# Third batch's attention eight slots earlier, second batch's queries loaded one slot earlier, and memory traffic ordered behind TensorE steps

## The chip, the cores and the metric

One Trainium2 chip, of which the kernel uses one core. The metric is the device time of one execution in microseconds (us), the median of three runs for the kernel before. The engines are named as in the profile: PE is TensorE with PEld its weight loads, DVE is VectorE, ACT is ScalarE, POOL is GpSimd, and SP is SyncE, which here only issues DMAs.

## The reference

Three stages follow one another; all of it is float32, with the weights of the second stage handed over as 64-bit numbers.

```python
q_s = exp(q - max(q, -1)); q_s = q_s / (sum(q_s, -1) + 1e-9)      # over the head's 64
k_s = exp(k - max(k, 2));  k_s = k_s / (sum(k_s, 2) + 1e-9)       # over the sequence
kv  = einsum('bhsd,bhse->bhde', k_s, v)
x   = einsum('bhsd,bhde->bhse', q_s, kv)     # -> (2304, 512)
x   = (((x @ w1) * (x @ w2)) @ w3) @ w_out   # 512->1024, 1024->1024, 1024->512
p   = probs / (probs.sum(-1) + 1e-9)
out = sum over 4 experts e of p[:, e] * (relu(x @ e1[e]) @ e2[e])
```

Batch is 4, heads 8, sequence 576, head dimension 64, so x has 2304 rows (tokens) of 512.

## The kernel before

**Numbers.** TensorE multiplies in a reduced 32-bit format (fp32r), so every large product is made of three: high part by high part, high by low, low by high. `mm3` (L107 to L110) issues the three. `split` (L101) makes the parts: a rounding copy on ACT (L102), then the remainder on DVE (L103).

**Phase one, to about 442 us.** The tokens are worked in five chunks: four of 512 and one of 256. The work is written as numbered slots, and each slot issues one step on TensorE with what was put `before`, `mid` and `after` it:

- Slots 0 to 5: attention of batch 0. Per pair of heads, `k_max` (L202 on: maxima on DVE, two transposes on PE at L212 and L216, copy `mx` on ACT at L220), one slot later `k_exp` (L233 on ACT), then `k_v` (PE L245, copy `bd` on ACT L257). Per query group, `q_exp` (maximum on DVE L266; difference L281 on DVE and one exponential L285 on ACT), `q_norm`, and `q_turn` (transposes on PE L313, copy `qT` on ACT L315). `x_stage` (PE L326, ACT L342 and L347) writes x into the chunk's tiles. The second group of batch 1 is in `ON_SCALAR`: its exponentials are 18 small activations on ACT, each with its own maximum and its own sum (L274).
- Slots 6 to 13: `ab_step(0, f)`, f = 0 to 7: x @ w1 and x @ w2 of chunk 0 for one eighth of the columns, 24 matmuls of 512 columns. `convert(f + 2)` stands ahead of each.
- Slots 14 to 21: the same for chunk 1, with one `unit` of w3 @ w_out beside each; slots 22 to 29: the remaining units, and `h_step`, which splits the products (w1 part `ah`, L479) into `h`.
- Slots 30 to 45: `y_step` of chunks 0 and 1; from slot 46 (`REST`) `ab_step`, `h_step` and `y_step` of chunk 2, then of chunks 3 and 4 together.

The first columns of w1 and w2 that a step uses come from a conversion pair: `load_to` fetches two 512 KB pieces as pairs of 32-bit words into one of 4 buffers, `conv_abs` takes the magnitude on ACT (L123), `conv_rest` makes a float of it in four DVE operations (L127 to L138), and `split` writes the tile `wg`. There are 20 pairs; a raw tile's name is `f_...` in the orders below. Chunk 0 uses the tiles straight from the conversion; `save_w12` (L443) writes them to DRAM, and `load_w12` (L448) reads them again for the later chunks.

Two tables place the attention of the later batches: `K_SLOT` and `Q_SLOT` give the slot of each `k_max` and `q_exp`; keys and values are loaded three slots earlier, queries two. From slot 33 on a further generator, `cooking`, prepares the expert weights of the last stage: it loads raw tiles (L584), adds and subtracts quarters on DVE (`minus`, L588), splits each result into a tile `eo` and saves it (L608). `cook_some(k)` advances it by k of 99 steps.

**What sets the order.** All instructions of an engine form one queue. A scheduler fills the queues from a modelled timeline, taking program order as a priority, so an instruction can move ahead of others. `hold(key, inst)` (L117) adds, for the scheduler alone, that `inst` comes behind the instructions noted in `gate[key]`; it makes no semaphore, so on the chip nothing waits for it. The DMAs of phase one all stand in SP's queue.

**Phase two, from 442 us.** 24 groups of `layer1` (PE L879) and `layer2` (PE L953) over the four experts, with prepared weights `eg` read back from DRAM (L670).

## Time and profile before

| what | value |
| --- | --- |
| runs | 1160.33, 1161.68, 1163.48 us; median 1161.68 us |
| the profiled execution | 1162.17 us, of which the span (first to last instruction) 1160.4 us |
| mean granted TensorE clock in it | 0.996 of full speed (full is 2.4 GHz) |
| PE busy | 1127.0 us, 97% of the span |
| DVE busy | 868.4 us, 75% |
| ACT busy | 534.7 us, 46% |
| POOL busy | 46.8 us, 4% |
| chain that ended last | PE 86%, DVE 6%, DMA 5%, SP's queue 2% |

A busy share says how long an engine had an instruction running. Where PE is busy for all of a stretch, only fewer or faster matmuls shorten it; where it has gaps, the entry beside an instruction names the gap before it and what ended it. Such an entry reads `[3.06 <-DVE mt L214]`: 3.06 us idle, ended by the DVE instruction of line 214 on tile `mt`. The line numbers are those of the kernel before.

### The profile page before, as it was taken

Reading aid. Unit: us, or ns where it says so; the run is one execution under the profiler, and the core shown is the slowest. Engines: PE = TensorE matmul, PEld = TensorE weight load, DVE = VectorE, ACT = ScalarE, POOL = GpSimd, SP = SyncE. Lnnn points to the kernel's source line nnn. Section 1 sums busy time; section 2 is a strip of 40 time slices with the busy share of each in tenths; the row PEclk is TensorE's granted clock in tenths of the full one; section 3 lists DMA queues with packets and bytes.
Section 4 is the critical chain, followed back from the end, with each engine's and each line's share of the span. In section 5 each row is a group of like instructions: output and inputs, shape, how many; then the busy total and the mean of one; then the engine's idle time right before and its main releaser. Section 6 shows DMA issues by size and latency. Waiting matters only on the chain.

```text
span 1160.4 us, 18707 instructions
## 1 busy us (share of the span) xinstructions
PE 1127.0 (97%) x7048; PEld 1050.2 (91%) x7048; DVE 868.4 (75%) x1428; ACT 534.7 (46%) x982; POOL 46.8 (4%) x70
## 2 busy tenths in 40 slices
PE   5889999999999999999999999999999999999997
PEld 4667888787888889999999999999999999999997
DVE  7898866766457414999989987777779877777777
ACT  4665535555445315555555544433336344433441
POOL 0012300103000000000000000000000000000000
PEclk9999999999999999999999999999999999999999
DMA  9999960599799746777877888777777797777773
GB/s 238 264 352 305 372 233 1 183 381 405 282 378 356 277 164 224 288 286 283 295 275 273 287 303 307 251 251 251 250 249 257 244 305 256 248 253 249 241 262 111
DMA packets 127418, 310.12 MB, mean 267 GB/s; under 512 B 31968, under 2 KB 52960, under 8 KB 127328
## 3 DMA queue, kind: packets, MB, share of 16 engines
q1 hardware_dynamic: 126848, 308.14, 76.9%
q8 instruction: 56, 0.92, 0.3%
q10 hardware_dynamic: 480, 0.79, 0.2%
q14 instruction: 34, 0.28, 0.1%
HBM read 232.33 MB, written 76.55 MB: 266 GB/s over the span
## 4 chain that ended last, share of the span: by engine, by line
PE 86%; DVE 6%; DMA 5%; SPq 2%; issue 1%; ACT 1%; DVEq 0%; ACTq 0%
PE hp L879 28%; PE op L953 26%; PE ab L110 5%; PE ab L108 5%; PE ab L109 5%; PE y L108 3%; PE y L110 2%; PE y L109 2%; DMA kr<-in_k_dram 2%; DVE acc L937 2%; PE kv L245 2%; PE W L108 1%; PE W L109 1%; PE W L110 1%; DVE h L103 1%; DVE blk L588 1%
## 5 line engine op out<-in xcount | busy, mean ns | idle before, releaser
L953 PE MATMUL op<-eg,h 128*128 128x256 f32 x3024 | 379.9, 280 | 0.5 <-DMA eg<-e_b 0.4
L879 PE MATMUL hp<-t,eg 128*128 128x384 f32 x2016 | 377.1, 336 | 1.1 <-DVE acc L937 0.9
L953 PEld LDWEIGHTS op<-eg,h 128*128 128x128 f32 x3024 | 373.4, 188 | 1.0 <-PE hp L879 0.7
L879 PEld LDWEIGHTS hp<-t,eg 128*128 128x128 f32 x2016 | 344.6, 188 | 3.3 <-DVE acc L937 2.1
L937 DVE SCALAR_TENSOR_TENSOR acc<-op,prob,acc 128x256 f32<-128x256 f32 (+1 forms) x396 | 197.2, 527 | 43.1 <-PE op L953 43.1
L102 ACT ACTIVATE h<-blk 128x768 fp32r<-128x768 f32 x168 | 138.0, 842 | 144.5 <-DVE blk L588 108.2
L103 DVE TENSOR_TENSOR h<-blk,h 128x768 fp32r<-128x768 f32 x168 | 157.2, 950 | 24.4 <-ACT h L102 24.3
L862 ACT ACTIVATE blk<-hp 128x384 f32<-128x384 f32 x192 | 90.7, 490 | 138.8 <-PE hp L879 137.1
L866 DVE TENSOR_TENSOR blk<-hp,blk 128x384 f32<-128x384 f32 x144 | 79.3, 556 | 66.8 <-PE hp L879 63.6
L108 PE MATMUL ab<-x,wg 128*128 128x512 f32 (+1 forms) x320 | 121.1, 381 | 3.4 <-ACT wg L102 2.7
L109 PE MATMUL ab<-x,wg 128*128 128x512 f32 (+1 forms) x320 | 119.3, 373 | 0.2 <-ACT x L347 0.2
L110 PE MATMUL ab<-x,wg 128*128 128x512 f32 (+1 forms) x320 | 119.3, 375 | 0.0
L868 ACT ACTIVATE blk<-blk 128x768 f32<-128x768 f32 x72 | 60.6, 845 | 73.6 <-DVE blk L866 72.0
L588 DVE TENSOR_TENSOR blk<-blk 128x768 f32<-128x768 f32 x96 | 91.4, 952 | 0.5
L108 PEld LDWEIGHTS ab<-x,wg 128*128 128x128 f32 x320 | 60.8, 191 | 14.6 <-ACT wg L102 3.5
L109 PEld LDWEIGHTS ab<-x,wg 128*128 128x128 f32 x320 | 61.0, 191 | 10.8 <-ACT x L347 0.8
L110 PEld LDWEIGHTS ab<-x,wg 128*128 128x128 f32 x320 | 61.0, 191 | 10.8 <-DVE wg L103 0.5
L480 DVE TENSOR_TENSOR ah<-ab,ah 128x512 f32<-128x512 f32 (+1 forms) x40 | 25.4, 635 | 51.1 <-PE ab L110 46.5
L103 DVE TENSOR_TENSOR eo<-e2r,eo 128x512 fp32r<-128x512 f32 x56 | 41.6, 744 | 19.1 <-ACT eo L102 18.7
L109 PE MATMUL y<-h,W 128*128 128x512 f32 x128 | 50.3, 395 | 0.0
L110 PE MATMUL y<-h,W 128*128 128x512 f32 x128 | 49.4, 392 | 0.0
L108 PE MATMUL y<-h,W 128*128 128x512 f32 x128 | 47.9, 404 | 0.0
(98 smaller groups left out, 1037.2 us busy)
## 6 DMA issues: line engine op xcount, KB each, us to landing
eg<-e_t SPq DMA_DIRECT2D x96, 512.0 KB, 4.5
eg<-e_b SPq DMA_DIRECT2D x72, 512.0 KB, 4.8
eg<-e_s SPq DMA_DIRECT2D x68, 512.0 KB, 4.4
eg<-e_a SPq DMA_DIRECT2D x51, 512.0 KB, 4.6
wg<-w SPq DMA_DIRECT2D x48, 512.0 KB, 8.4
f<-in_moe_w_dram SPq DMA_DIRECT2D x32, 512.0 KB, 6.5
e_t<-eo SPq DMA_DIRECT2D x32, 512.0 KB, 6.3
e_s<-eg SPq DMA_DIRECT2D x28, 512.0 KB, 4.8
```

Of the source, the lines that this page charges most:

```text
L102: i = nc.scalar.activation(out=hi, in_=src, func=ACTF.Copy)
L103: j = eng.tensor_tensor(out=lo, in0=src, in1=hi.bitcast(F32), op=ALU.subtract)
L108: nc.tensor.matmul(out=ps, lhsT=w_hi, rhs=r_hi, start=first, stop=False, **kw)
L109: nc.tensor.matmul(out=ps, lhsT=w_hi, rhs=r_lo, start=False, stop=False, **kw)
L110: nc.tensor.matmul(out=ps, lhsT=w_lo, rhs=r_hi, start=False, stop=last, **kw)
L588: return lambda: nc.vector.tensor_tensor(out=dst, in0=x, in1=y, op=op)
L862: nc.scalar.activation(out=block(name)[:, u], in_=src, func=func)
L866: nc.vector.tensor_tensor(out=x[:, u], in0=src, in1=x[:, u], op=ALU.add)
L868: nc.scalar.activation(out=x, in_=x, func=ACTF.Relu)
L879: nc.tensor.matmul(out=q, lhsT=w[:, sw, kt, P * u:P * u + P], rhs=t[b][:, kt, st], start=new and kt == 0 and i == 0, stop=kt == 1 and i == ...
L937: nc.vector.scalar_tensor_tensor(out=dst, in0=src, scalar=prob[:, T, e:e + 1], in1=dst, op0=ALU.mult, op1=ALU.add,)
L953: nc.tensor.matmul(out=q[:, c:c + DH], lhsT=g[:, sh, u, P * i:P * i + P], rhs=w[:, sw, u], start=new and u == 0 and j == 0, stop=u == 1 an ...
```

## The change

- The third batch's keys (`K_SLOT[2]`) go from slots 30 to 36 to slots 22 to 28, its queries from 30 and 34 to 22 and 26. Its loads move with them (three and two slots ahead), and are ordered behind the last conversion instruction of the thirteenth pair (n == 12).
- The second batch's queries are loaded three slots ahead instead of two.
- The fourth batch's loads are put at fixed slots (25 to 31 and 24, 28) and ordered behind the last matmul of the latest `ab_step` or `y_step`, which `gate["pace"]` holds (`mm3` now returns it).
- The reloads of w1 and w2 for chunks 2 and later, the splits, the additions and the saves of `cooking` are ordered behind that matmul too. Before, the splits alone were ordered behind one `h_step` (key "cook").
- Beside the y steps `cook_some(1)` becomes `cook_some(2)`, and `cook_some` first flushes the saves that wait.

```diff
-K_SLOT = [[0, 0, 0, 0], [6, 7, 8, 9], [30, 32, 34, 36], [46, 47, 48, 50]]
-Q_SLOT = [[2, 2], [6, 8], [30, 34], [46, 48]]
+K_SLOT = [[0, 0, 0, 0], [6, 7, 8, 9], [22, 24, 26, 28], [46, 47, 48, 50]]
+Q_SLOT = [[2, 2], [6, 8], [22, 26], [46, 48]]
...
-        nc.tensor.matmul(out=ps, lhsT=w_lo, rhs=r_hi, start=False, stop=last, **kw)
+        return nc.tensor.matmul(out=ps, lhsT=w_lo, rhs=r_hi, start=False, stop=last, **kw)
...
-        nc.sync.dma_start(
+        hold("pace" if b > 2 else ("in", b), nc.sync.dma_start(
...
-                put(before, s - 2, load_q, b, j)
+                put(before, Q_SLOT[2][j] + 2 if b > 2 else s - (3 if b == 1 else 2), load_q, b, j)
...
-                put(before, s - 3, load_kv, b, hp)
+                put(before, K_SLOT[2][i] + 3 if b > 2 else s - 3, load_kv, b, hp)
...
+            if n == 12:
+                gate["in", 2] = [last]
...
+            if c > 1:
+                hold("pace", gate["dma"][0])
...
-                mm3(
+                gate["pace"] = [mm3(
...
-        lo = split(h[:, 0, 0:n], h[:, 1, 0:n], prods[c, f // 2][:, f % 2, 0:n])[1]
-        if (c, f) == (0, 3):
-            gate["cook"] = [lo]
+        split(h[:, 0, 0:n], h[:, 1, 0:n], prods[c, f // 2][:, f % 2, 0:n])
...
+    def cook_flush():
+        while len(waiting) > 2:
+            hold("pace", save_e(*waiting.pop(0)))
...
-                        hold("cook", i)
+                        hold("pace", i)
...
-                do()
-                while len(waiting) > 2:
-                    save_e(*waiting.pop(0))
+                i = do()
+                if i is not None:
+                    hold("pace", i)
...
     def cook_some(k):
+        cook_flush()
...
-            cook_some(1)
+            cook_some(2)
```

The `hold` around the load stands at each DMA of `load_k`, `load_v` and `load_q`. The following rows are the built programs' queues at three places. No time is in them.

**SP, the loads of the second batch's first tiles.** `qr`, `kr` and `vt` are raw queries, keys and values; `f64` is the raw tile of a conversion pair. Before:

```order
L410 DMA f64_270<-in_moe_w2_dram 128x4x256
L169 DMA kr_302<-in_k_dram 128x2x256
L172 DMA kr_302<-in_k_dram 64x2x64
L180 DMA vt_305<-in_v_dram 128x4x64 x2
L183 DMA vt_305<-in_v_dram 64x2x64
L410 DMA f64_273<-in_moe_w1_dram 128x4x256
L410 DMA f64_273<-in_moe_w2_dram 128x4x256
L196 DMA qr_402<-in_q_dram 64x2x576 x2
L169 DMA kr_405<-in_k_dram 128x2x256
```

And with the change:

```order
L412 DMA f64_270<-in_moe_w2_dram 128x4x256
L198 DMA qr_302<-in_q_dram 64x2x576 x2
L169 DMA kr_305<-in_k_dram 128x2x256
L172 DMA kr_305<-in_k_dram 64x2x64
L182 DMA vt_308<-in_v_dram 128x4x64
L412 DMA f64_273<-in_moe_w1_dram 128x4x256
L412 DMA f64_273<-in_moe_w2_dram 128x4x256
```

The queries (two DMAs) stood behind the first keys and values and a whole conversion pair, and now stand ahead of them all.

**ACT, beside the third and fourth steps of chunk 0.** `qe` are the exponentials of the second batch's second query group, `wg` from `f_497` is a weight tile of the third step and from `f_579` one of the fourth, `ah` the third step's product copy. Before:

```order
L315 ACTIVATE qT<-qt 128x2x192 x3
L274 ACTIVATE qe,qs<-qr,qm 128x64 x12
L102 ACTIVATE wg<-f_497 128x512 x2
L274 ACTIVATE qe,qs<-qr,qm 128x64 x6
L220 ACTIVATE mx<-mt 128x128
L479 ACTIVATE ah<-ab 128x512
L257 ACTIVATE bd<-kv,rs 64x64 x2
L102 ACTIVATE wg<-f_579 128x512 x2
L123 ACTIVATE f_681<-f_421 128x512 x2
```

And with the change:

```order
L317 ACTIVATE qT<-qt 128x2x192 x3
L276 ACTIVATE qe,qs<-qr,qm 128x64
L102 ACTIVATE wg<-f_497 128x512 x2
L276 ACTIVATE qe,qs<-qr,qm 128x64 x17
L222 ACTIVATE mx<-mt 128x128
L485 ACTIVATE ah<-ab 128x512
L259 ACTIVATE bd<-kv,rs 64x64 x2
L123 ACTIVATE f_681<-f_424 128x512 x2
L102 ACTIVATE wg<-f_579 128x512 x2
```

Eleven of the twelve exponentials that stood ahead of the third step's weights now stand behind them, and the next pair's magnitudes (`f_681`) have passed the fourth step's weights.

**SP, where chunk 2's weights are read again.** `wg<-w_0` and `wg<-w_1` are the reloads for the first two steps of chunk 2, `e_...<-eo` the saves of prepared expert weights, `e2r` a raw expert tile. Before:

```order
L584 DMA e2r<-in_moe_w_dram 128x2x512 x2
L608 DMA e_0_t_2604<-eo 128x1024
L608 DMA e_1_b_2609<-eo 128x1024
L608 DMA e_1_b_2686<-eo 128x1024
L608 DMA e_1_b_2756<-eo 128x1024
L608 DMA e_1_t_2787<-eo 128x1024
L448 DMA wg<-w_0_674 128x1024
L448 DMA wg<-w_0_676 128x1024
L448 DMA wg<-w_1_785 128x1024
L448 DMA wg<-w_1_787 128x1024
```

And with the change:

```order
L588 DMA e2r<-in_moe_w_dram 128x2x512 x2
L612 DMA e_0_s_2261<-eo 128x1024
L612 DMA e_0_b_2263<-eo 128x1024
L612 DMA e_0_b_2298<-eo 128x1024
L612 DMA e_0_b_2316<-eo 128x1024
L452 DMA wg<-w_0_674 128x1024
L452 DMA wg<-w_0_676 128x1024
L612 DMA e_0_t_2340<-eo 128x1024
L452 DMA wg<-w_1_785 128x1024
L612 DMA e_0_t_2342<-eo 128x1024
L452 DMA wg<-w_1_787 128x1024
```

Ten saves of expert tiles stand ahead of the first reload where eighteen stood, and the four reloads have saves between them.

## Rows read from the trace of the kernel before

**Rows 1.** The page's first part: busy time (share of the span) x instructions, by engine.

```profile
PE 1127.0 (97%) x7048; PEld 1050.2 (91%) x7048; DVE 868.4 (75%) x1428; ACT 534.7 (46%) x982; POOL 46.8 (4%) x70
```

**Rows 2.** Windows by stage: window, length, busy PE, PEld, DVE, ACT, POOL (xinstructions), PEclk, DMA share, GB/s.

```profile
29.00:58.00 29.00, 23.84 (x103) 17.77 (x102) 24.64 (x44) 19.75 (x52) 0.95 (x5) 0.94 1.08 264
58.00:87.00 29.00, 24.99 (x114) 18.84 (x113) 28.15 (x49) 18.16 (x63) 3.63 (x4) 0.94 1.07 352
87.00:116.00 29.00, 26.58 (x119) 20.39 (x119) 24.08 (x34) 17.19 (x46) 7.46 (x9) 1.00 0.99 305
145.00:174.00 29.00, 29.00 (x133) 23.96 (x133) 19.38 (x28) 11.14 (x22) 2.38 (x3) 1.00 0.70 234
```

**Rows 3.** Waits of PE, 29 to 145 us: engine line <- releaser: us in total, times, longest.

```profile
PE ab L108 <- ACT wg L102: 2.7, 2, 2.5
PE xp L343 <- ACT x L342: 2.3, 5, 0.8
```

**Rows 4.** Windows, as rows 2: PE's two long waits, and the stretch behind each.

```profile
42.90:45.90 3.00, 0.00 (x0) 0.00 (x0) 3.00 (x5) 0.80 (x4) 0.00 (x0) 1.00 0.86 194
45.90:49.30 3.40, 3.40 (x11) 2.91 (x12) 3.22 (x8) 1.79 (x5) 0.00 (x0) 0.50 0.99 316
66.10:68.60 2.50, 0.01 (x1) 0.00 (x0) 2.35 (x3) 2.50 (x14) 2.50 (x1) 1.00 1.03 412
69.80:73.20 3.40, 3.35 (x9) 2.63 (x9) 3.12 (x10) 3.36 (x14) 0.00 (x0) 0.50 1.12 328
```

**Rows 5.** Timeline of PE: start, duration, engine, line, operation, tile, shapes, count [idle before <-releaser].

```profile
45.91 0.79 PE L216 MATMUL mt<-ident,mt 128*128 128x128 f32 x2 [3.06 <-DVE mt L214]
...
68.60 0.50 PE L108 MATMUL ab<-x,wg 128*128 128x512 f32 x1 [2.50 <-ACT wg L102]
...
77.63 0.50 PE L108 MATMUL ab<-x,wg 128*128 128x512 f32 x1
...
87.47 0.53 PE L343 MATMUL xp<-x,nident 128*128 128x288 f32 x2 [0.79 <-ACT x L342]
...
265.07 0.88 PE L313 MATMUL qt<-ident,qe 128*128 128x128 f32 x6 [1.07 <-ACT mx L220]
...
265.70 0.47 PE L108 MATMUL ab<-x,wg 128*128 128x512 f32 x1
...
442.03 2.07 PE L879 MATMUL hp<-t,eg 128*128 128x384 f32 x11
```

**Rows 6.** Timeline of DVE, columns as rows 5.

```profile
42.69 1.35 DVE L266 TENSOR_REDUCE qm<-qr 128x18 f32<-128x1152 f32 x1 [3.27 <-DMA qr<-in_q_dram]
...
63.12 1.21 DVE L138 SCALAR_TENSOR_TENSOR f<-f,f 128x1024 int32<-128x1024 int32 x1
...
402.33 0.68 DVE L103 TENSOR_TENSOR eo<-e2r,eo 128x512 fp32r<-128x512 f32 x1
```

**Rows 7.** Timeline of ACT, columns as rows 5.

```profile
63.95 0.34 ACT L274 ACTIVATE qe<-qr,qm 128x64 f32<-128x64 f32 x1
...
67.60 0.34 ACT L274 ACTIVATE qe<-qr,qm 128x64 f32<-128x64 f32 x1
...
67.94 1.14 ACT L102 ACTIVATE wg<-f 128x512 fp32r<-128x512 f32 x2
...
71.13 0.58 ACT L479 ACTIVATE ah<-ab 128x512 f32<-128x512 f32 x1
71.61 0.62 ACT L257 ACTIVATE bd<-kv,rs 64x64 f32<-64x64 f32 x2
...
73.31 1.22 ACT L123 ACTIVATE f<-f 128x512 f32<-128x512 f32 x2
...
85.77 1.15 ACT L285 ACTIVATE qe<-qr 128x1152 f32<-128x1152 f32 x1
```

**Rows 8.** Timeline of SP's queue: start of the issuing, its duration, line, DMA.

```profile
254.23 2.82 SPq L448 DMA_DIRECT2D wg<-w  x4
```

**Rows 9.** The page's sixth part: DMA issues, xcount, KB each, median us from issue to landing.

```profile
wg<-w SPq DMA_DIRECT2D x48, 512.0 KB, 8.4
```

More of the change, by code (lines that the diff above doesn't have):

```diff
@@ L168, in load_k @@
         src = k[b, 2 * hp:2 * hp + 2]
-        nc.sync.dma_start(
+        hold("pace" if b > 2 else ("in", b), nc.sync.dma_start(
             out=t[:, :, 0:KR], in_=src[:, 0:KR * P].rearrange("h (p r) d -> p h r d", p=P)
-        )
-        nc.sync.dma_start(out=t[0:KX, :, KR], in_=src[:, KR * P:S].rearrange("h p d -> p h d"))
+        ))
+        hold("pace" if b > 2 else ("in", b), nc.sync.dma_start(
+            out=t[0:KX, :, KR], in_=src[:, KR * P:S].rearrange("h p d -> p h d")
+        ))
         kraw[b, hp] = t
@@ L179, in load_v @@
         for h in range(2):
-            nc.sync.dma_start(
+            hold("pace" if b > 2 else ("in", b), nc.sync.dma_start(
                 out=t[:, h, 0:KR, 0:D], in_=src[h, 0:KR * P].rearrange("(p r) d -> p r d", p=P)
-            )
-        nc.sync.dma_start(
+            ))
+        hold("pace" if b > 2 else ("in", b), nc.sync.dma_start(
             out=t[0:KX, :, KR, 0:D], in_=src[:, KR * P:S].rearrange("h p d -> p h d")
-        )
+        ))
         vt[b, hp] = t
@@ L195, in load_q @@
             h0 = 4 * hh + 2 * j
-            nc.sync.dma_start(
+            hold("pace" if b > 2 else ("in", b), nc.sync.dma_start(
                 out=t[QP * hh:QP * hh + QP],
                 in_=q[b, h0:h0 + 2].rearrange("h (p r) d -> p h r d", p=QP),
-            )
+            ))
         qraw[b, j] = t
@@ L472, in ab_step @@
                 o = P * kt
-                mm3(
+                gate["pace"] = [mm3(
                     ps[:, 0:n], gw[i][:, 0, o:o + P], gw[i][:, 1, o:o + P],
                     xa.at(c, kt, 0), xa.at(c, kt, 1), x == 0, x == KT - 1,
-                )
+                )]
             pss.append(ps)
@@ L506, in y_step @@
             o = P * d
-            mm3(
+            gate["pace"] = [mm3(
                 yps[c, d], Wg[f][:, 0, o:o + P], Wg[f][:, 1, o:o + P],
                 h[:, 0, 0:n], h[:, 1, 0:n], f == 0 and not (pair and d % 2), f == NF - 1, pair,
-            )
+            )]
     yd = dr.tile([P, KT, NT], F32, name="yd")
@@ L607, in save_e @@
         ewd[kind, n, name] = d = dr.tile([P, 2, 2, 256], F32, name=f"{kind}_{n}_{name}")
-        nc.sync.dma_start(out=d, in_=g.bitcast(F32))
+        return nc.sync.dma_start(out=d, in_=g.bitcast(F32))
     COOKED = [("e1", n) if i == 0 else ("e2", n) for n in range(NE1) for i in range(2)]
     COOKED += [("e2", n) for n in range(NE1, NGE)]
+    waiting = []
+    def cook_flush():
+        while len(waiting) > 2:
+            hold("pace", save_e(*waiting.pop(0)))
     def cooking(pool):
-        raws_e, waiting = {}, []
+        raws_e = {}
         def ask(i):
@@ L634, in cooking @@
             for do in cook(kind, n, raws_e.pop(i), part_of(kind, n)):
-                do()
-                while len(waiting) > 2:
-                    save_e(*waiting.pop(0))
+                i = do()
+                if i is not None:
+                    hold("pace", i)
                 yield
         while waiting:
-            save_e(*waiting.pop(0))
+            hold("pace", save_e(*waiting.pop(0)))
     def load_y(p):
```

## The prediction

> **What bounds the kernel now.** I read the shares first. PE is busy for 97% of the span [rows 1]: 1127.0 of 1160.4 us, so 33.4 us of gaps are all that an order can win by filling them, plus whatever PE runs at half its clock. The change adds and removes no matmul. So I look for the stages that hold those gaps, by windows [rows 2]. From 29 to 58 us PE is busy for 23.84 of 29 us, from 58 to 87 for 24.99, from 87 to 116 for 26.58; from 145 to 174 it is busy for all 29.00. The gaps that the change can reach therefore lie in the stage where chunk 0 is multiplied while weights are still converted and the second batch's attention runs. Two of these windows also show a mean granted clock of 0.94. From 442.03 us [rows 5] phase two runs on the same order as before, and I cost it at nothing.
>
> Who is waited for says the view of waits and PE's timeline. The first long gap is 3.06 us before 45.91 us, ended by DVE's maximum `mt` [rows 5]; DVE itself had waited 3.27 us for the second batch's queries [rows 6]. The second is 2.50 us before 68.60 us, ended by ACT's copy of the weight tile `wg` [rows 5]. Behind each the clock falls: the 3.40 us from 45.90 and the 3.40 us from 69.80 have a granted clock of 0.50 [rows 4], that is 1.2 of 2.4 GHz. PE did in each half of what it would have done, so each such stretch costs 1.7 us. The waits with ACT's `x` as releaser make 2.3 us over five times, the longest 0.8 [rows 3].
>
> **The second batch's queries.** The loads now stand ahead of the first keys, the values and a conversion pair in SP's queue. The maximum of the queries no longer blocks DVE, but the key maximum behind it then waits for keys that are issued later than before by two query DMAs, and PE's gap ends with the chain key maximum, transpose, `mt`. The gap can shrink by 3.06 with its clock stretch of 1.7 behind it (4.8 in all), or by nothing. I take 0.4, near the lower end: the stage's DMA share is already 1.08 [rows 2], so the keys will not come much sooner. **+0.4 us.**
>
> **The exponentials of its second group.** ACT started the first of twelve at 63.95 and the last at 67.60, then `wg` at 67.94 [rows 7]: 4.0 us that the third step of chunk 0 waited out. DVE had the float ready when its last conversion ended, 63.12 + 1.21 = 64.33 [rows 6]. Now one exponential stands ahead, so `wg` starts at about 64.5; before, PE started 0.66 us behind it (68.60 against 67.94), so the third step starts at about 65.2 instead of 68.6. But the exponentials do not vanish. Seventeen follow at (67.60 - 63.95) / 11 = 0.33 us, 5.6 us in all. ACT has `wg` done at 64.5 + 1.14 = 65.7, the exponentials at 71.3, then `ah` 0.58, `bd` 0.62 and the magnitudes 1.22 [rows 7], which the new order puts ahead of the fourth step's `wg`: 73.7. PE can take it 0.66 later, at 74.4. The third step and the attention beside it took 77.63 - 68.60 = 9.0 us, 7.3 without the half-clock loss, and so end at 72.5. PE then waits 1.9 us, and the fourth step starts at 74.4 against 77.63. **+3.2 us** with the queries' 0.4 in it, so 2.8 of its own.
>
> **The clock behind the new wait.** No row shows a wait of 1.9 us in this stage. A wait of 2.50 was followed by 3.40 us at 0.50, one of 0.79 was not followed by a fall: the window from 87 to 116 has 1.00 [rows 2, 5]. 1.9 is nearer to 2.50, so I take one stretch, **-1.7 us**, between 0 and -1.7.
>
> The Trainium skill speaks against this choice: "TensorE: Matmul & The Clock Gate", section "HAM oscillation — how this bites in real kernels", lays a fall of the clock to long waits, such as those for a transfer, and not to short ones. If it counts this wait among the short, the stretch would not be paid and the sum would stand 1.7 us better, which is the near end of the first rival below. This trace has a fall behind the 2.50 us wait [rows 4], so I keep the row.
>
> **The third batch out of this stage.** Its query exponential of 1.15 us [rows 7] started at 85.77, in front of the copy of `x` for which PE waited 0.79 before 87.47 [rows 5]. The exponential goes to a later slot; the wait goes nearly whole: **+0.8 us**, between 0 and 1.15. Its DVE work goes too: DVE was busy for 28.15 of 29 us [rows 2], but PE's waits for `wg` other than the long one come to 2.7 - 2.5 = 0.2 us [rows 3]: **+0.2 us**.
>
> **Where it goes.** Slots 22 to 29. From 145 to 174 us DVE is busy for 19.38 of 29 us, ACT for 11.14, and the DMA engines have a share of 0.70 against 1.08 and 1.07 before [rows 2]. The attention's matmuls cost there what they cost where they stood, since PE was full in both places; the price is 0 as long as DVE's 9.6 us of slack per window cover what conversions and attention now share. Gone, it is rival three's kind of loss. The wait of 1.07 us before 265.07 [rows 5], where PE stood for a copy in the middle of attention, falls away in the stage with new room: **+1.07 us**, between 0 and 1.07.
>
> **The expert weights.** Cooking is ordered later, and ends later. Its last tile was written at 402.33 [rows 6] and phase two needs the first at 442.03 [rows 5]; about 18 us later it still has 20 us to be saved and read. The rate of two steps per y step gives some back. Cost 0, covered by those 40 us.
>
> **The sum.** 0.4 + 2.8 - 1.7 + 0.8 + 0.2 + 1.07 = 3.6 us. Against the profiled execution, 1162.17 - 3.6 = 1158.6. That execution stands 0.49 above the median of 1161.68, so the forecast is **1158.1 us**. A change of 0.3%, 3.5 us, is what measuring tells from none: faster means below 1158.2, slower above 1165.2. The forecast sits on the lower of these bounds.
>
> **Rival one: the stage opens further.** The new wait is too short to bring the clock down, or is not there at all, as the exponentials find gaps. Without the clock stretch the gain is 5.3 and the time 1156.4. With both long waits and both stretches gone, 3.06 + 1.7 + 2.50 + 1.7 + 0.8 + 0.2 + 1.07 = 11.0, it is 1150.7. For it: the 0.79 wait without a fall, and that DVE loses the third batch's work. Against: the 18 exponentials still take ACT 6 us in front of one step or the next. Chance 0.24.
>
> **Rival two: the wait only moves.** The order of ACT shifts, but the fourth step pays what the third is spared: the held operations only change places, as no semaphore stands behind the order, and the 17 exponentials, the copies and a second clock stretch take the 2.8 back. What is left is under 0.5: 1161.2 us. For it: ACT was busy for all 2.50 us of the wait [rows 4], so it is ACT's work that is short of room, and none of the second batch's is removed. Chance 0.20.
>
> **Rival three, slower: chunk 2's first weights come late.** Before, their reload was issued at 254.23 [rows 8] and first used at 265.70 [rows 5], 11.5 us ahead; such a load takes 8.4 us at the median [rows 9]. That leaves 3.1 us. The reload is now ordered behind a TensorE step and stands in SP's queue behind saves that wait for DVE's splits, with more saves between the four. It decides when the issue slips by more than 3.1 us; every microsecond beyond is lost by PE. With the lead all gone it costs 8.4 us against the gain of 3.6: 1161.68 + 4.8 = 1166.5. Against: PE's queue is full ahead of it, so the matmul it is ordered behind may lie early. Chance 0.16.
>
> **How the numbers follow.** Forecast 0.40, rivals 0.24, 0.20 and 0.16. The forecast's own spread is skewed to more gain by its bounds, so about 0.26 of its 0.40 lies below 1158.2 and 0.14 within. Faster: 0.26 + 0.24 = 0.50; the same: 0.14 + 0.20 = 0.34; slower: 0.16. The range reaches from the first rival's far end to the third's price: 1150.5 to 1166.5.
>
> **What would show it.** Right: `wg` of the third step starting near 64.5, one PE wait for `wg` of about 2 us some 7 us later with a clock of 0.50 behind it, the wait before 45.91 shorter by under a microsecond, no 0.79 wait behind a third-batch exponential, and everything from 145 us on shifted by about 3 us. Wrong: a wait for `f` or `wg` between 145 and 203 us, with DVE full; a PE wait for the reloaded `wg` ahead of chunk 2; or a wait for `eg` at the start of phase two.

## The result, and the profile after

The changed kernel took 1171.35 us (median of 4 runs, 1170.65 to 1176.07) against 1161.24 us of the kernel before. The ratio is 1.0095, with a 95% interval of 1.0077 to 1.0113: slower by about 10 us, where 3.6 us less had been forecast. The profiled execution took 1171.51 us, its span 1169.7 us; the span grew by 9.3 us. The slots are earlier in the program, but the ordering behind the thirteenth pair makes the third batch later on the chip: POOL's first subtraction for it began at 65.96 us before and begins at 149.65 us now.

The windows of the kernel after, with the columns of [rows 2], tell where:

```profile
29.00:58.00 29.00, 24.55 (x109) 17.78 (x108) 26.59 (x49) 19.95 (x52) 1.05 (x5) 1.00 1.12 281
58.00:87.00 29.00, 26.42 (x132) 20.39 (x131) 22.98 (x41) 22.14 (x75) 0.55 (x4) 1.00 0.82 302
87.00:116.00 29.00, 26.34 (x113) 19.82 (x113) 20.18 (x26) 13.93 (x35) 0.73 (x4) 1.00 0.71 259
...
145.00:174.00 29.00, 27.02 (x116) 21.95 (x116) 26.35 (x30) 10.65 (x19) 9.63 (x5) 0.94 1.02 251
174.00:203.00 29.00, 22.68 (x93) 17.92 (x92) 24.90 (x33) 13.59 (x28) 8.55 (x6) 0.82 0.19 46
203.00:232.00 29.00, 28.14 (x137) 22.18 (x136) 14.53 (x30) 13.86 (x32) 7.05 (x10) 1.00 0.41 119
...
261.00:290.00 29.00, 29.00 (x139) 24.08 (x138) 15.44 (x27) 13.30 (x24) 3.09 (x2) 1.00 1.01 393
```

And the kernel before, for two windows that [rows 2] does not have:

```profile
174.00:203.00 29.00, 29.00 (x134) 23.92 (x133) 18.81 (x26) 16.42 (x31) 0.20 (x1) 1.00 0.00 1
203.00:232.00 29.00, 28.98 (x131) 23.02 (x130) 21.71 (x35) 16.13 (x33) 4.47 (x4) 1.00 0.53 182
```

The stage to 87 us became better, and better than forecast: PE is busy for 24.55 and 26.42 us, against 23.84 and 24.99 [rows 2], and the mean clock is 1.00 in both, where it was 0.94. But PE was full from 145 to 203 us before; now it has gaps of 1.98 us in the first of the two windows and 6.32 us in the second, and the clock drops. POOL, which was busy for 2.38 us [rows 2] and 0.20 us there, is now busy for 9.63 and 8.55.

PE's timeline names the gaps; the first two rows answer to the third and fourth step of chunk 0 in [rows 5], the last to chunk 2's first step:

```profile
63.85 0.50 PE L108 MATMUL ab<-x,wg 128*128 128x512 f32 x1
...
72.30 0.50 PE L108 MATMUL ab<-x,wg 128*128 128x512 f32 x1 [0.21 <-ACT wg L102]
...
167.97 0.69 PE L108 MATMUL ab<-x,wg 128*128 128x512 f32 x1 [1.98 <-DVE ah L486]
...
186.44 0.50 PE L108 MATMUL W<-wg 128*128 128x512 f32 x1 [1.19 <-DVE ah L486]
...
192.66 1.22 PE L110 MATMUL W<-wg 128*128 128x512 f32 x2 [5.13 <-DVE wg L103]
...
274.41 0.48 PE L108 MATMUL ab<-x,wg 128*128 128x512 f32 x1
```

PE waits for DVE three times, for the product `ah` and for the low part of a weight tile `wg`. So I read DVE's timeline of that stretch, and beside it POOL's. DVE first:

```profile
159.09 3.57 DVE L134 SCALAR_TENSOR_TENSOR f<-f,f 128x1024 int32<-128x1024 int32 x1
...
163.85 1.21 DVE L138 SCALAR_TENSOR_TENSOR f<-f,f 128x1024 int32<-128x1024 int32 x1
164.98 2.33 DVE L207 TENSOR_TENSOR m<-kr 128x256 f32<-128x256 f32 x1
167.24 0.68 DVE L486 TENSOR_TENSOR ah<-ab,ah 128x512 f32<-128x512 f32 x1
...
183.68 2.16 DVE L301 TENSOR_SCALAR qs<-qs 128x18 f32<-128x18 f32 x1
185.71 0.67 DVE L486 TENSOR_TENSOR ah<-ab,ah 128x512 f32<-128x512 f32 x1
186.31 1.33 DVE L268 TENSOR_REDUCE qm<-qr 128x18 f32<-128x1152 f32 x1
...
187.81 5.39 DVE L103 TENSOR_TENSOR wg<-f,wg 128x512 fp32r<-128x512 f32 x2
```

And POOL: differences (L283 of queries, L232 of keys) and the multiplication by the reciprocal sums (L303). Each batch has two query groups, so two L283 and two L303:

```profile
149.65 2.22 POOL L283 TENSOR_TENSOR qr<-qr,qm 128x1152 f32<-128x1152 f32 x1 [41.19 <-DMA kr<-in_k_dram]
157.19 2.30 POOL L232 TENSOR_TENSOR kr<-kr,mx 128x512 f32<-128x512 f32 x2 [5.32 <-ACT mx L222]
159.45 2.12 POOL L303 TENSOR_TENSOR qe<-qe,qs 128x1152 f32<-128x1152 f32 x1
164.00 3.03 POOL L283 TENSOR_TENSOR qr<-qr,qm 128x1152 f32<-128x1152 f32 x1 [2.43 <-DMA vt<-in_v_dram]
183.50 2.26 POOL L283 TENSOR_TENSOR qr<-qr,qm 128x1152 f32<-128x1152 f32 x1 [16.47 <-DVE qm L268]
185.71 0.11 POOL L179 MEMSET vt<- 128x10 f32 x1
185.77 2.14 POOL L232 TENSOR_TENSOR kr<-kr,mx 128x512 f32<-128x512 f32 x2
187.87 2.11 POOL L283 TENSOR_TENSOR qr<-qr,qm 128x1152 f32<-128x1152 f32 x1
189.94 2.11 POOL L303 TENSOR_TENSOR qe<-qe,qs 128x1152 f32<-128x1152 f32 x1
```

The L283 at 149.65 and 164.00 are the third batch's, and so are both L303 and the L232. The L283 at 183.50 and 187.87 are the fourth batch's: two such rows remain, near 181 and 186 us, in the version below that has nothing of the third batch on POOL. In the kernel before the same two began at 101.83 and 136.98 us, so the change brought them here as well.

The two timelines are to be read side by side. L134 takes 3.57 us where the same operation took 1.21 to 1.23 elsewhere: it ends at 162.66, about one usual duration after POOL's L303 ended at 161.57. L207 takes 2.33 us instead of 0.41 and ends just behind POOL's L283 (167.03). L301, a tiny operation of 0.16 us elsewhere, takes 2.16 and ends with another L283. The two subtractions for `wg`, 1.28 us together elsewhere, take 5.39 us: the first begins at 187.81, just ahead of L283, and they get done only once L283 and L303 have ended at 192.05. So a DVE instruction that waits is not let in between two POOL operations that follow one another directly: L134 began while L232 ran (to 159.49) and waited for L303 too. Each of PE's three gaps stands behind one of these, the second behind an operation of the fourth batch. Counting each DVE instruction that is over 0.15 us longer than the shortest of its line and shape, there are six from 145 to 203 us, 13.0 us longer together (the expectations below put it at 12.2); the kernel before has none there.

The gaps also cost clock. The windows around the first and the last:

```profile
167.90:171.50 3.60, 3.53 (x9) 2.75 (x10) 2.28 (x5) 2.52 (x5) 0.00 (x0) 0.53 1.00 271
187.50:192.60 5.10, 0.03 (x1) 0.00 (x0) 5.10 (x5) 0.31 (x1) 4.55 (x3) 0.61 0.01 2
192.60:201.50 8.90, 8.84 (x26) 7.05 (x27) 6.54 (x13) 2.17 (x6) 0.00 (x0) 0.65 0.11 33
```

That is 3.60 x 0.47 = 1.7 us behind the first and 8.90 x 0.35 = 3.1 us behind the last. With the gaps of 1.98 + 6.32 us and 0.84 us less PE work from 203 to 232 us (28.14 against 28.98 before), this stage costs 13.9 us more. Against it stand 5.6 us won before 145 us: 2.1 us of gaps (9.7 us left between 29 and 145 us, where there were 11.8), 3.4 us of clock, and 0.1 us ahead of 29 us. And 1.07 us won from 261 to 290 us, where PE is now full. That leaves 7.2 of the 9.3 us. Of the rest, some 2 us, a part lies in the stage itself: measured against the usual duration of its matmuls (the PE loss of the next section) it costs 15.2 us, since the windows count short delays between matmuls as busy. Behind 319 us PE's gaps grew by only 0.23 us to 442 us and by 0.35 us from there to 580 us; a single named wait of it, for a prepared weight at 476.80 us, grew from 0.41 to 0.74 us.

### The profile page after: what moved, and what is told of

It reads as the page before. It is cut to its first block, busy times and chain, and to the rows that moved or that the text cites. A ratio compares the mean times of both kernels' runs of the same rounds, so it can differ in the third digit from the quotient of the medians.

```text
span 1169.7 us, 18719 instructions
## 1 busy us (share of the span) xinstructions
PE 1130.1 (97%) x7048; PEld 1050.4 (90%) x7048; DVE 870.4 (74%) x1428; ACT 534.9 (46%) x982; POOL 44.4 (4%) x70
## 4 chain that ended last, share of the span: by engine, by line
PE 86%; DVE 5%; DMA 3%; ACT 2%; issue 1%; SPq 1%; DVEq 0%; ACTq 0%
PE hp L890 29%; PE op L964 27%; PE ab L108 5%; PE ab L110 5%; PE ab L109 5%; PE y L109 3%; PE y L108 3%; PE y L110 2%; PE kv L247 1%; DVE acc L948 1%; DMA vt<-in_v_dram 1%; DMA eg<-e_b 1%; PE W L110 1%; PE xp L328 1%; PE W L108 1%
## 5 line engine op out<-in xcount | busy, mean ns | idle before, releaser
L948 DVE SCALAR_TENSOR_TENSOR acc<-op,prob,acc 128x256 f32<-128x256 f32 (+1 forms) x396 | 196.9, 526 | 43.2 <-PE op L964 43.0
```

Of the source, the lines that this page charges most:

```text
L948: nc.vector.scalar_tensor_tensor(out=dst, in0=src, scalar=prob[:, T, e:e + 1], in1=dst, op0=ALU.mult, op1=ALU.add,)
```

## The experiments

Each experiment is a version of the kernel before or of the changed kernel. One caution holds for all: the scheduler fills the queues anew for every edit, so a version differs from its neighbour in order too. I therefore read in each where PE waits, beside the total. "PE loss" below is PE's time above the usual duration of its matmuls, summed over a stretch, which takes in gaps and half clock alike: from 0 to 145 us 41.6 before and 36.0 after, from 145 to 232 us 1.8 before and 17.0 after.

### The third batch put back

```diff
-K_SLOT = [[0, 0, 0, 0], [6, 7, 8, 9], [22, 24, 26, 28], [46, 47, 48, 50]]
-Q_SLOT = [[2, 2], [6, 8], [22, 26], [46, 48]]
+K_SLOT = [[0, 0, 0, 0], [6, 7, 8, 9], [30, 32, 34, 36], [46, 47, 48, 50]]
+Q_SLOT = [[2, 2], [6, 8], [30, 34], [46, 48]]
-put(before, Q_SLOT[2][j] + 2 if b > 2 else s - (3 if b == 1 else 2), load_q, b, j)
+put(before, s - (3 if b == 1 else 2), load_q, b, j)
-put(before, K_SLOT[2][i] + 3 if b > 2 else s - 3, load_kv, b, hp)
+put(before, s - 3, load_kv, b, hp)
-            if n == 12:
-                gate["in", 2] = [last]
```

> The changed kernel with the third batch's slots, its ordering behind the thirteenth pair and the fourth batch's load slots put back; the early queries of the second batch, the ordering behind TensorE steps and the faster cooking stay. Stage theory: the change lost 15 us of PE time between 145 and 232 us and won 5.6 us before 145, so putting the batch back gives 1171.4 - 15 plus up to 5.6 of lost gain: 1157 to 1162, and no PE wait over 1 us between 145 and 232. Rival (the ordering behind TensorE steps and the cooking delay conversions and weights): the waits between 145 and 203 stay, 1168 to 1172.

Measured: 1174.03 us, ratio 1.0093 (1.0077 to 1.0109). The total missed the stage theory's number and is nearer to the rival's, above which it lies, but not for the rival's reason. PE loss from 145 to 232 us is 2.2 us, as the stage theory had it. The time went elsewhere: the gain before 145 us is gone (43.2 us), and a loss of 12 us stands from 232 to 319 us, where the kernel before has gaps of 1.07 us and this one of 6.31: the fourth batch's POOL work now meets the splits of `h`. PE's gap there, then DVE's and POOL's rows under it:

```profile
280.46 0.80 PE L109 MATMUL y<-h,W 128*128 128x512 f32 x1 [2.30 <-DVE h L103]
```

```profile
277.81 2.60 DVE L103 TENSOR_TENSOR h<-ah,h 128x512 fp32r<-128x512 f32 x1
```

```profile
277.30 2.56 POOL L303 TENSOR_TENSOR qe<-qe,qs 128x1152 f32<-128x1152 f32 x1
```

It is the same picture in another place: a split of 0.68 us took 2.60 while POOL multiplied.

### The third batch moved off POOL

```diff
-ON_VECTOR = {(x, b, i) for x in "esm" for b in range(2) for i in range(4)}
+ON_VECTOR = {(x, b, i) for x in "esm" for b in range(3) for i in range(4)}
```

This edit is on the changed kernel. `ON_VECTOR` lists what runs on DVE: the differences of keys ("e") and of queries ("s") and the multiplication ("m"), by batch. What it does not list runs on POOL, so in both kernels POOL does this work for the third and fourth batch; L281 on DVE, as the kernel before was described, holds for the first two batches alone.

> The changed kernel with the third batch's six kinds of differences and multiplications on DVE, where they ran on POOL. Theory that POOL's tensor operations hold DVE up (12.2 us of lengthened DVE instructions between 145 and 203 us): DVE bears some 9 us of its own (1.35 for each of four query operations, about 0.9 for each of four key differences) and loses the 12.2 of lengthening; no DVE subtraction for wg takes over 0.8 us, the 5.1 us wait is gone or under 2, 1159 to 1167. Rival (DVE simply has too much work of its own in this stage, POOL does not matter): 9 us more on DVE make it worse, 1172 to 1180.

Measured: 1162.69 us, ratio 0.9998 (0.9987 to 1.0009). DVE was given more work and the kernel became 9 us faster than the change. The rival, too much work on DVE, would have made it slower. The windows:

```profile
145.00:174.00 29.00, 29.00 (x134) 23.99 (x133) 26.34 (x40) 11.72 (x22) 0.00 (x0) 1.00 1.02 261
174.00:203.00 29.00, 28.04 (x133) 22.36 (x132) 28.87 (x44) 16.01 (x33) 4.47 (x4) 1.00 0.31 74
```

PE is full in the first. DVE is busy for 26.34 us there as against 26.35 us in the changed kernel: it now does 4.8 us of the batch's operations itself, and had been held up for 6.9. The same busy share stood for work in one kernel and partly for standing still in the other. One detail of the expectation failed: a subtraction for `wg` still took 2.55 us, at 185.94 us, beside the fourth batch's L283.

### The third batch's POOL work left out

```diff
-            either("e", b, hp).tensor_tensor(
-                out=x, in0=x, in1=mx[0:p].to_broadcast([p, 2, n, D]), op=ALU.subtract
-            )
+            if b != 2:
+                either("e", b, hp).tensor_tensor(
+                    out=x, in0=x, in1=mx[0:p].to_broadcast([p, 2, n, D]), op=ALU.subtract
+                )
...
```

The same condition stands before the query difference and the multiplication.

> The changed kernel without the third batch's differences and its multiplication by the reciprocal sum (left out: k minus max, q minus max, and the division of q's exponentials, of that batch alone), that is without POOL's 18 us of work between 145 and 203 us; DVE's own instructions all stay. Theory that POOL holds DVE up: PE's waits of 1.98, 1.19 and 5.13 us and their clock stretches go, 1155 to 1160. Rival (DVE's own work): the waits stay, 1167 to 1172.

Measured: 1162.3 us, ratio 1.0 (0.9988 to 1.0011). The three gaps are gone; the largest left between 145 and 232 us is 0.87 us. The total is 2 us above the range, and the reason is a useful bound: even with this work absent the stage from 145 to 232 us loses 6.6 us, 4.8 more than before. So the third batch's POOL work accounts for some 10 of the 15 us. The 5 us left are not all its other work: the fourth batch's two L283 still run here (4.81 us from 182.90 us), two subtractions for `wg` beside them take 3.74 us, and the wait of 0.87 us stands behind these. The expectation counted POOL's 18 us of work from 145 to 203 us as the third batch's; 4.4 us of it are the fourth's.

### The third batch behind the last conversion

```diff
-            if n == 12:
+            if n == 19:
-K_SLOT = [[0, 0, 0, 0], [6, 7, 8, 9], [22, 24, 26, 28], [46, 47, 48, 50]]
-Q_SLOT = [[2, 2], [6, 8], [22, 26], [46, 48]]
+K_SLOT = [[0, 0, 0, 0], [6, 7, 8, 9], [31, 33, 35, 37], [46, 47, 48, 50]]
+Q_SLOT = [[2, 2], [6, 8], [31, 35], [46, 48]]
```

The fourth batch's loads stand three and two slots ahead of its own steps, as before.

> The changed kernel with the third batch's loads ordered behind the twentieth and last conversion pair instead of the thirteenth, its slots at 31 to 37 and 31, 35 and the fourth batch's loads three and two slots ahead of its own steps. If the loss is the meeting of this batch with the last conversions, it goes and the gain before 145 us (5.6 us) stays: 1154 to 1158. If the loss is any third-batch work on an otherwise full PE, or the ordering behind TensorE steps: 1166 to 1172.

Measured: 1180.99 us, ratio 1.0154 (1.0135 to 1.0172). A miss, and the slowest version of all. It was to avoid the conversions, and it did: PE loss from 145 to 232 us is 4.5 us. But from 232 to 319 us it is 22.5 us. The attention's short matmuls came one behind another with small gaps and, in the window below, at half the clock; then a split of `h` came late and PE waited 3.81 us for it:

```profile
240.00:248.00 8.00, 6.76 (x20) 4.60 (x21) 1.47 (x7) 3.04 (x10) 1.99 (x4) 0.50 0.00 0
```

```profile
286.63 2.08 PE L108 MATMUL y<-h,W 128*128 128x512 f32 x4 [3.81 <-ACT h L102]
```

Moving the batch later is no cure, then: the conversions are not the only work that DVE must deliver on time.

### The third batch's move alone

The edit is the kernel before with the two slot rows of the third batch and the ordering of its loads behind the thirteenth pair, nothing else of the change.

```diff
-K_SLOT = [[0, 0, 0, 0], [6, 7, 8, 9], [30, 32, 34, 36], [46, 47, 48, 50]]
-Q_SLOT = [[2, 2], [6, 8], [30, 34], [46, 48]]
+K_SLOT = [[0, 0, 0, 0], [6, 7, 8, 9], [22, 24, 26, 28], [46, 47, 48, 50]]
+Q_SLOT = [[2, 2], [6, 8], [22, 26], [46, 48]]
+            if n == 12:
+                gate["in", 2] = [last]
...
-        nc.sync.dma_start(
+        hold(("in", b), nc.sync.dma_start(
...
```

> The kernel before with the third batch's slots and the ordering of its loads behind the thirteenth pair alone; the second batch's queries, the fourth batch's loads, the cooking and the reloads as before. If the third batch's meeting with the last conversions is the whole cause: waits for wg or ah of over 1 us between 145 and 203 us, DVE instructions lengthened by some 12 us there, 1165 to 1173. If the loss needs the fourth batch's early loads or the ordering behind TensorE steps: no such wait, 1155 to 1161.

Measured: 1174.85 us, ratio 1.0104 (1.0074 to 1.0134). That is just above the range: the move is enough by itself. A wait of 1.93 us for `ah` stands at 191.13 us, DVE instructions are lengthened by 8.6 us from 145 to 203 us (some 12 were expected) and by 4.4 more to 232. The two long waits of the kernel before are there, near 47 and 71 us (3.50 us, where it was 3.06, and 2.50), so the gain before 145 us does not come from the third batch's leaving alone. Part of the 12.6 us that this version loses lies there too: from 29 to 87 us the clock is 0.88, where it was 0.94.

### The early queries alone

```diff
-                put(before, s - 2, load_q, b, j)
+                put(before, s - (3 if b == 1 else 2), load_q, b, j)
```

> The kernel before with only the second batch's queries loaded one slot earlier. If the gain of 5.6 us that the change has before 145 us comes from this: 1155 to 1157, with no 2.50 us wait for wg near 68 us. If it comes from the third batch's leaving that stage: 1160 to 1162, with a wait for wg of over 2 us between 60 and 80 us.

Measured: 1163.08 us, ratio 1.0008 (0.9994 to 1.0021): no difference, and neither theory had it whole. The 2.50 us wait for `wg` is gone, as the first said, but the time is not better, as the second said. PE loss before 145 us is 43.5 us: other waits, of 0.78, 0.98 and 0.92 us between 73 and 101 us, stand in its place. With the run before this means that the gain needs both: the queries early, and the third batch out of the stage. Both are not enough for all of it: the versions that keep both and take POOL work off the later batches have by the same measure 2 to 3 of the 5.6 us. In the version with the third batch on DVE, PE waits 2.81 us before its query transposes at 40.60 us, where the changed kernel waits 1.70, and the clock falls. The rest of the 5.6 came with the order of that one build.

### The third batch off POOL in the kernel before

```diff
-ON_VECTOR = {(x, b, i) for x in "esm" for b in range(2) for i in range(4)}
+ON_VECTOR = {(x, b, i) for x in "esm" for b in range(3) for i in range(4)}
```

> The kernel before with the third batch's differences and multiplications on DVE instead of POOL. In the kernel before these POOL operations lie between 58 and 145 us, where DVE was busy for 28.15 of 29 us in one window and its instructions were lengthened by 8.7 us in all. Theory that POOL holds DVE up about as long as it runs: DVE gets 9 us of its own for 8.7 of lengthening, no difference: 1158 to 1164. Rival (POOL runs beside DVE at nearly no cost, and the loss in the change has another cause): DVE's 9 us more come on top in a full stage, 1166 to 1172.

Measured: 1164.08 us, ratio 1.0019 (1.0006 to 1.0033), just outside the first range and far from the rival's. Nine microseconds more on a full DVE cost some 2 us, and from 58 to 145 us DVE is as busy as before, 78.08 against 78.26 us.

### Both later batches off POOL

```diff
-ON_VECTOR = {(x, b, i) for x in "esm" for b in range(2) for i in range(4)}
+ON_VECTOR = {(x, b, i) for x in "esm" for b in range(4) for i in range(4)}
```

This edit is on the changed kernel.

> The changed kernel with the differences and multiplications of the third and the fourth batch on DVE; POOL keeps only its fills. With the third batch alone there the time was 1162.7, with 4.0 us of lengthened DVE instructions between 174 and 203 us, beside the fourth batch's POOL work, and 6.3 us of PE time lost between 174 and 232. If POOL is the cause there too, half of that or more goes: 1156 to 1161. If DVE, busy for 28.87 of 29 us there, is short of time anyway: 1162 to 1168.

Measured: 1159.91 us, ratio 0.9975 (0.9961 to 0.9990): faster than the kernel before by about 2.9 us, the one version that beats both. The windows:

```profile
145.00:174.00 29.00, 29.00 (x134) 24.02 (x133) 25.85 (x39) 11.46 (x22) 0.00 (x0) 1.00 1.01 256
174.00:203.00 29.00, 28.38 (x135) 22.44 (x134) 28.97 (x48) 17.37 (x36) 0.23 (x2) 1.00 0.35 80
```

DVE is busy for 28.97 of 29 us in the second, and PE still for 28.38. From 58 to 232 us no DVE instruction is over 0.15 us longer than the shortest of its line and shape. A full DVE that is not held up keeps PE fed; the changed kernel's DVE, busy for 24.90 us there, did not.

### The same, with the queries back

```diff
-put(before, Q_SLOT[2][j] + 2 if b > 2 else s - (3 if b == 1 else 2), load_q, b, j)
+put(before, Q_SLOT[2][j] + 2 if b > 2 else s - 2, load_q, b, j)
```

This edit is on the version just above.

> The changed kernel with the third and fourth batch's differences and multiplications on DVE (1159.9 us), and the second batch's queries loaded two slots ahead again. If the early queries give the gain before 145 us that remained after the third batch left: the 2.50 us wait for wg near 68 us comes back with its clock stretch, 1161 to 1165. If the third batch's leaving is enough, and the early queries only bring the wait of 2.7 us before 40.4 us: 1156 to 1160.

Measured: 1170.16 us, ratio 1.0061 (1.0042 to 1.0081). Slower than either range. The 2.50 us wait came back near 68.56 us, as the first theory said, but that is the smaller part. Most is a loss of 11.7 us from 145 to 232 us, with POOL doing nothing but fills. DVE's timeline, then PE's:

```profile
185.23 1.35 DVE L268 TENSOR_REDUCE qm<-qr 128x18 f32<-128x1152 f32 x1 [3.00 <-DMA qr<-in_q_dram]
186.50 1.22 DVE L134 SCALAR_TENSOR_TENSOR f<-f,f 128x1024 int32<-128x1024 int32 x1
...
187.97 0.69 DVE L486 TENSOR_TENSOR ah<-ab,ah 128x512 f32<-128x512 f32 x1
```

```profile
188.71 0.50 PE L108 MATMUL W<-wg 128*128 128x512 f32 x1 [3.11 <-DVE ah L486]
```

The maximum of the fourth batch's first query group waited for its queries for 3.00 us, with a conversion and the product behind it in DVE's queue; SP issued their load at 176.38 us, where the version above did at 168.11. So POOL is not the only way in which these batches hold DVE up: a load that comes late does it as well. It also shows what the order alone can cost, 10 us between two versions in which POOL only fills, so the sizes that single versions give to POOL are rough; the rows of lengthened instructions are not touched by this.

### The cooking put back

The changed kernel with the splits ordered behind one `h_step` as before, one cooking step beside a y step, and reloads and saves without an order.

```diff
-            cook_some(2)
+            cook_some(1)
-                        hold("pace", i)
+                        hold("cook", i)
-            if c > 1:
-                hold("pace", gate["dma"][0])
...
```

> The changed kernel with the cooking's pace (one step beside a y step), its order behind one h step, and the free reloads of w1 and w2 put back; the third and fourth batch's slots and the early queries stay. If the loss lies where the third batch's POOL work meets the conversions, this alters nothing there: 1169 to 1174, with a wait of several us for wg between 145 and 203. Rival (ordering the weight traffic behind TensorE steps costs the time): 1157 to 1163.

Measured: 1172.17 us, ratio 1.0083 (1.0058 to 1.0109). Nothing is gained; the waits stand where they stood, 2.73 us at 188.87 and 4.34 us at 195.07 us. The ordering of this traffic behind TensorE steps is not the cause.

### Queries or keys

```diff
+ON_VECTOR |= {(x, 2, i) for x in "sm" for i in range(4)}
```

```diff
+ON_VECTOR |= {("e", 2, i) for i in range(4)}
```

The first line puts the third batch's query operations on DVE, the second, in a version of its own, its key differences.

> The changed kernel with the third batch's four query operations (L283, L303) on DVE and its key differences (L232) left on POOL. In the changed kernel the DVE instruction ahead of each of PE's three waits was lengthened under a POOL operation on queries (L134 and L207 before 167.97 us, L301 before 186.44, L103 before 192.66, under 2.1 to 3.0 us of L283 or L303 each time). If it is those, the three waits go and the time is 1159 to 1165. If any third-batch work in this stage does it, 1169 to 1174.

> The counterpart: the third batch's key differences (L232) on DVE, its four query operations left on POOL. If the query operations on POOL are what holds DVE up: long DVE instructions under them stay, and waits of over 1 us for wg or ah between 145 and 203 us, 1166 to 1173. If the key differences are: 1158 to 1165.

Measured: 1164.55 us (ratio 1.0020, 1.0008 to 1.0032) with the queries on DVE and 1166.43 us (1.0041, 1.0028 to 1.0054) with the keys there. Both lie inside the range of the query theory, the second at its lower edge, so each half alone gives back a good part; it is not the queries only. With the queries on DVE no wait from 145 to 203 us is over 1 us; with the keys there one of 1.77 us for `ah` stays, at 185.20 us. What stays on POOL still holds DVE up. With the queries on DVE, DVE's longest row, and then POOL's row beside it:

```profile
186.67 2.95 DVE L104 TENSOR_TENSOR wg<-f,wg 128x512 fp32r<-128x512 f32 x1
```

```profile
186.96 2.11 POOL L284 TENSOR_TENSOR qr<-qr,qm 128x1152 f32<-128x1152 f32 x1
```

That POOL row is of the fourth batch's queries, which this version left there. Line numbers are one higher than in the changed kernel.

## Why the prediction was wrong

**The step that failed** is the one headed "Where it goes": "the price is 0 as long as DVE's 9.6 us of slack per window cover what conversions and attention now share". It measured 13.9 us. The condition was named, and "a wait for `f` or `wg` between 145 and 203 us, with DVE full" was named as what would show it wrong, but it was given no chance of its own. Three things were wrong with it. The third batch's differences and multiplications run on POOL, and I costed only what the batch does on DVE, ACT and PE; nor did I see that the fourth batch's query differences come along. PE was not "full in both places": where the batch stood, [rows 2] has PE busy for 24.99 and 26.58 of 29 us. And slack summed over a window says nothing on when DVE is held up: PE lost 8.3 us in gaps although DVE was idle for 2.65 and 4.10 us of the two windows.

The sign was in the trace of the kernel before. In its DVE timeline an operation that takes 0.69 us otherwise took 1.92 beside a POOL multiplication of 3.65 us:

```profile
128.04 1.92 DVE L127 TENSOR_SCALAR f<-f 128x1024 f32<-128x1024 f32 x1
130.00 0.69 DVE L130 TENSOR_SCALAR f<-f 128x1024 int32<-128x1024 int32 x1
```

```profile
125.77 3.65 POOL L301 TENSOR_TENSOR qe<-qe,qs 128x1152 f32<-128x1152 f32 x1 [1.15 <-ACT wg L102]
```

By the count used above, nine DVE instructions were lengthened from 58 to 145 us there, 6.6 us together. PE had gaps in that stage anyway, so little of it need have reached PE; that is argued, but giving this work to DVE in the kernel before made it no faster. The move put the same POOL work where PE was full.

The Trainium skill has the rule that I should have weighed: "SBUF — State Buffer", section "SBUF: two separate sides", says that VectorE and GpSimd share one pair of ports, held for a whole instruction by whichever starts first, and that on VectorE's side it concerns operations with two inputs in SBUF or in a faster two-port mode. The rows agree: L134, L207 and the subtraction for `wg` (5.39 us) have two such inputs and were held up, while the reduction L268, with one input, took its usual 1.33 us beside POOL's L232, and the product `ah`, with one input in PSUM, its usual 0.67. L301 and L127 have one input and were held up too; whether they ran in such a mode no row shows. On who comes first the rows say more than the rule: L134 and the subtraction at 187.81 start ahead of the POOL operations that hold them longest (159.09 against 159.45, 187.81 against 187.87), each while an earlier POOL operation still ran.

**The other terms.**

- The early queries (+0.4): undersized. The gap of 3.06 us became one of 1.70 before 39.64 us, and its clock stretch of 1.7 us is gone.
- The exponentials (+2.8): the mechanism was right. One exponential stands ahead of `wg`, which ACT begins at 62.52 us, 2 us sooner than I had it, as the queries came sooner; 17 follow. The fourth step starts at 72.30, forecast 74.4. The new wait came out as 0.21 us for `wg` and 0.56 us for an attention copy, not 1.9: the attention's matmuls took their place in the gap.
- The clock behind the new wait (-1.7): there was none, the window has 1.00. So the first rival's condition came true in this stage. Its nearer price, 5.3 us less the 1.07 of another stage, has 4.2 us for this one; it gave 5.6, 3.4 of them clock. The wait itself was mis-sized, so the choice between the two rows was never put to the test.
- The third batch out of the stage (+0.8, +0.2): the wait of 0.79 us went, and no wait over 0.35 us is left for `x` before 100 us. But waits of 0.56 us for `x` and 0.71 for `wg` stand near 110 us, and from 87 to 116 us PE is busy for 26.34 us against 26.58: no gain there.
- The wait near 265 us (+1.07): as forecast; the window from 261 to 290 us is full.
- The sum: the 3.2 us of the exponentials were worked out from unshifted rows, so the queries' 0.4 was not in them, and taking it off left the sum 0.4 too small. The first rival's far end is 1150.7, not the range's 1150.5.
- The expert weights (0): their last tile was written at 429.5 us instead of 403.0, and phase two began without waiting for them.
- The third rival: the reload was issued at 262.67 us and first used at 274.41, 11.7 us ahead, as before (11.5). No wait. The slower outcome came by another way.

Of the 5 us or so that the stage lost even without the third batch's POOL work, a part is the fourth's: with both batches off POOL, PE's gaps from 145 to 232 us come to 1.46 us, against 2.37 there and 9.16 in the changed kernel. That the rest comes from DVE's fuller queue is argued from its windows, and no run separates it from the new order.

## What to carry to other kernels

Before moving work into a stage, list every engine that it runs on, and look what each does to its neighbours there: find an instruction on DVE that ran beside POOL's work and compare it with its usual duration. A busy share cannot tell work from being held up, and the slack that is read from it says neither when it comes nor what new holding up will take of it; it is an upper bound for what fits in. And a stage in which PE is full is the worst place to put such work, since each delay on the engine that feeds it becomes a gap, and a gap can take clock with it: here those of 1.98 and 5.13 us cost 1.7 and 3.1 us more. Last, look at what else the new order draws into the stage; here it was the next batch's work.

## What was not expected of the hardware

- A DVE operation beside POOL work can be lengthened by the whole of it, and by two POOL operations in a row: 0.16 us became 2.16, 1.28 us for two became 5.39.
- It holds in the other direction too: POOL's L283 began at 164.00 us beside DVE's L138, which ended at 165.06, and took 3.03 us instead of 2.11.
- Giving DVE 9 us more work left it as busy in one window as in the changed kernel (26.34 against 26.35 us) and made that kernel 9 us faster.
- The wait of 1.70 us before 39.64 us was followed by no fall of the clock, the one of 1.98 us before 167.97 by 3.60 us at 0.53.
